# Attention and two MLPs on one core: values of a group loaded by a thread of their own, pooled q and k first, a list ordered with other transfer times

## The chip, the cores and the metric

The kernel runs on one core of one Trainium2 chip. The metric is the device time of one execution in microseconds (us). The core's engines work side by side, each through its own list of instructions in order: TensorE (PE, the matrix products; PEld is its loading of the stationary operand), VectorE (DVE), ScalarE (ACT), GpSimd (POOL), and SyncE (SP, which here issues all DMA transfers). An instruction at the head of an engine's list that waits for another engine or a transfer holds up everything behind it in that list.

## The reference, cut to what matters

```python
# q, k, v: (4, 8, 576, 64); factor 4; scale 1/8
q_d, k_d, v_d = means over 4 neighbouring positions of q, k, v      # (4, 8, 144, 64)
out_up    = repeat(softmax(scale * q_d @ k_d.T) @ v_d, 4)           # pooled attention
scores    = where(abs(i - j) < 4, scale * q @ k.T, -1e9)            # local attention
x         = out_up + softmax(scores) @ v                            # -> (2304, 512)
for w_in, w_out in two layers:                                      # (512, 2048), (2048, 512)
    x = square(relu(x @ w_in)) @ w_out
```

The weights arrive as 64-bit floats. The kernel turns each into two 32-bit parts, a high and a low one, and makes each product of three: high by high, high by low, low by high.

## The kernel before, in words

The 2304 tokens are cut into 9 tiles of 256 (`TN`), the 2048 columns of the hidden layer into 8 parts of 256 (`NP`). A **step** (n, p) of a layer is 24 matmuls for `h` (L695) and 24 for `y` (L730; the second layer has 12 wide ones, L740). Layer 1 begins with tiles 0 and 1 interleaved, tile 1 two parts behind tile 0 (`LEAD`), so that each part of the weights is used twice as soon as it is there; the order starts h(0,0), h(0,1), y(0,0), h(0,2), y(0,1), y(0,2), h(1,0), h(0,3), y(1,0). ACT and DVE make `gH` and `gL` from `h` (L704 to L714) ahead of each y.

The input of layer 1 comes from the attention, for each of 4 batches `b`:

- `pool_qk` (L350), six times: load 384 KB of q or k (L356), add fours on POOL or DVE (L360, L362), transpose on PE (L368), move out by ACT.
- `pool_v` (L332), four times: load 288 KB of v (L337), add fours on POOL (L342, L346) into `vd`.
- `heads_of` (L377), four times, two head pairs at a time (`hd` has two buffers): scores (L389), maximum (L394), exponentials (L399), normalising (L405 to L409), transposes (L416), product with `vd` (L427), result into `outd`. The last product needs all four `pool_v`.
- `group` (L454), five times, 116 query rows each: load q and k rows (L468, two of 256 KB) and the values (L477, four of 64 KB, in pieces of 256 bytes), transposes (L484), masked scores (L499, L508), softmax (L518 to L533), transposes (L537), product with the values (L552), and the addition of the pooled part into the tile `xr` (L566). The product waits for all four `heads_of` of its batch. Tile 0 takes groups 0 to 2 of batch 0, tile 1 groups 2 to 4.

`convert` (L579) turns a quarter of a part of the weights into its two halves: load 512 KB into one of four `ld` buffers (L592 for `w_in`, L597 for `w_out`), ACT L607, DVE L609 and two L612, ACT again, and a subtraction on POOL or DVE (L621). There are 32 for each layer, four for each p, through two buffers `ga`. The `ld` buffers are shared with `pool_qk`, `pool_v`, the groups and the stores. While batch 0 is loaded, buffers of weights not yet filled stand in as more load, value and softmax buffers; rows call those `e`.

The order of all instructions on all engines is made once, when the program is built, by a planner (`Order`): each of the functions above is a thread that yields the engine and the duration it expects, or an event to wait for. Threads stand in lanes; a lane lets so many of its threads be live at a time, in order of a priority given in tiles. The planner starts whatever can start first by its own clock and writes the instruction down. `dma(nbytes)` is its price for a transfer, `dve`, `pool`, `act` those of the engines; where a step offers `[dve(...), pool(...)]` it takes the engine that would be done first. Until the first h it puts matmuls without use (L835, "fills") where it expects PE idle. So numbers in this planner set an order, and no instruction's duration on the chip. The lanes (L821 to L831) are:

```python
    o.lane(3, conversions(1, -0.7, 0.06))
    o.lane(4, groups)
    o.lane(4, heads)
```

Of the kernel before, what the change touches and what calls it, by code (L numbers as in the profile page):

```python
# [20 lines left out]
TN = 256  # L21
# [22 lines left out]
FT = 3  # L44

# [7 lines left out]
class Order:  # L53
# [72 lines left out]
    def run(self):  # L126
        while True:
# [21 lines left out]
            if eng == "SP":  # L149
                self.free[eng] = t + 0.46  # L150
                self.free["DMA"] = max(t + 1.1, self.free.get("DMA", 0.0)) + dur
                value = self.free["DMA"] + 0.95
            else:
                self.free[eng] = t + dur
                value = t + dur + LATENCY[eng]
# [48 lines left out]
def attention_two_mlp_kernel(  # L204
# [96 lines left out]

    def fast(cols):
        return "DVE", 0.165 + cols / 1920.0

    def pool(cols):
        return "POOL", 0.1 + cols * 0.0024
# [10 lines left out]
    def dma(nbytes):  # L317
        return "SP", nbytes / 360e3
# [13 lines left out]
    def pool_v(b, kh, j):  # L332
# [3 lines left out]
        yield dma(72 * 4096)  # L336
# [13 lines left out]
    def pool_qk(b, src, dst, c):  # L350
# [4 lines left out]
        yield dma(128 * 3072)  # L355
# [21 lines left out]
    def heads_of(b, hp):  # L377
# [30 lines left out]
        yield dve(576)  # L408
        nc.vector.tensor_tensor(out=p4, in0=p4, in1=sm.unsqueeze(2).to_broadcast([72, 4, GD]), op=ALU.mult)  # L409
# [32 lines left out]

    x_buf, x_left = {}, {t: TN for t in range(NT)}
# [9 lines left out]

    def group(b, i):  # L454
# [5 lines left out]
        blocks = []  # L460
        for c in range(2):
            qa = q0 + HQ * c
            blocks.append((c, qa, min(HQ, q0 + nq - qa), min(max(0, qa - 3), S - 64)))
        n = yield from f_ld.take(b == 0)
        raw = ld[n].bitcast(F32).rearrange("p (c e) -> p c e", c=2)
        for c, src in enumerate((q, k)):
            yield dma(128 * 2048)
            nc.sync.dma_start(  # L468
                out=raw[:, c].rearrange("p (h d) -> p h d", h=H), in_=src[b, :, r0:r0 + 128].rearrange("h s d -> s h d")
            )  # L470
        nv = yield from f_vw.take(b == 0)
        vw = vw_[nv]
        vj = v[b].rearrange("(h j) s d -> j s h d", j=2)
        for c, _, _, w0 in blocks:
            for j in range(2):
                yield dma(64 * 1024)
                nc.sync.dma_start(out=vw[64 * j:64 * j + 64, c], in_=vj[j, w0:w0 + 64])  # L477
# [25 lines left out]
        tt = yield "PE", 0.35  # L503
# [28 lines left out]
        yield [dve(512), pool(512)]  # L532
# [8 lines left out]
        pT = p.rearrange("p (h c) -> p h c", h=4)  # L541
        yield o.at("heads", b)
# [3 lines left out]
        tt = yield "PE", 0.7  # L546
# [9 lines left out]
        f_vw.put(nv, tt)  # L556
# [22 lines left out]
    def convert(layer, p, kind, half):  # L579
# [8 lines left out]
        if kind == 0:  # L588
            t = ld[n].rearrange("p (k f) -> p k f", k=2)
            fs, ks = slice(p * 256, p * 256 + 256), slice(2 * half, 2 * half + 2)  # L590
            yield dma(64 * 8192)
# [24 lines left out]
        if layer == 1:  # L616
# [3 lines left out]
            tt = yield [dve(512), pool(512)]  # L620
# [8 lines left out]
    def reload(p, kind):  # L629
# [13 lines left out]
        tt = yield [dve(1024), pool(1024)]  # L643
# [16 lines left out]
    def split_x():  # L660
        for n, (layer, t) in enumerate(seq):
# [8 lines left out]
            for c in range(2):  # L670
                ks = slice(2 * c, 2 * c + 2)
                tt = yield [dve(512), pool(512)]
# [135 lines left out]
    heads, groups = [], []  # L808
    for b in range(B):
        t = b * S / TN - 2  # L810
        heads += [(t - 0.1, pool_qk(b, s_, d_, c)) for c in range(3) for s_, d_ in ((q, qd), (k, kd))]
        heads += [(t, pool_v(b, kh, j)) for kh in range(2) for j in range(2)]
        heads += [(t + 0.05, heads_of(b, hp)) for hp in range(4)]
        groups += [((b * S + GQ * i) / TN - 1.9, group(b, i)) for i in range(NG)]
# [12 lines left out]
    o.lane(3, conversions(1, -0.7, 0.06))  # L827
    o.lane(4, groups)
    o.lane(4, heads)
# [60 lines left out]
```

## Time and profile before

| | |
|---|---|
| median of 3 runs | 1008.06 us (1007.47 to 1009.36) |
| the profiled execution, its own time | 1011.32 us |
| span in the profile, first to last instruction | 1009.5 us |
| PE busy | 966.9 us of the span |
| DVE, ACT, POOL busy | 375.9, 454.7, 190.1 us |
| mean granted TensorE clock | 0.981 |
| moved by DMA | 95.62 MB |

The profile's page gives busy times by engine, then 40 slices of the span with the busy share in tenths and the granted clock (PEclk, 9 is nearly full speed; full is 2.4 GHz). The trace can be asked for the busy times of any stretch, for the instructions in order of time, and for what ended each wait. POOL's spans are rough, and a busy PE may run at half clock or do fills, so that both must be looked at beside its busy time.

### The profile page before, as it was taken

The numbers are of one execution on the slowest core, as the hardware profiler recorded it, in microseconds if no ns is written. First come the engines' busy times: TensorE is split into PE (matmuls) and PEld (weight loads), VectorE is DVE, ScalarE is ACT, GpSimd is POOL, SyncE is SP. The second block draws the span as 40 slices with busy tenths as digits, with TensorE's granted clock in tenths as the row PEclk, the third lists the DMA queues.
The fourth block names the chain that finished last, engine by engine and source line by source line (L and its number), as shares of the span: only waits on it lengthen the run. The fifth ranks groups of instructions, "written<-read, shape, count | busy, mean of one in ns | idle before, by whom it ended". The sixth has DMA issues, their size and how long they took to land.

```text
span 1009.5 us, 19268 instructions
## 1 busy us (share of the span) xinstructions
PE 966.9 (96%) x8170; PEld 885.2 (88%) x8170; DVE 375.9 (37%) x651; ACT 454.7 (45%) x885; POOL 190.1 (19%) x170
## 2 busy tenths in 40 slices
PE   6788589999999999999999999999999999999998
PEld 4457589999999999999999998989898989898896
DVE  3698868534647668851111331111111111111110
ACT  3454666445655645543333663333333342424232
POOL 3666433323224101101000331101010100101000
PEclk9799799999999999999999999999999999999999
DMA  8665744326556557640000650101010010101000
GB/s 215 171 171 163 201 143 130 94 65 171 160 157 173 159 179 256 214 157 22 1 22 1 230 187 1 43 1 42 1 43 15 28 43 1 42 1 43 1 22 21
DMA packets 96966, 95.62 MB, mean 95 GB/s; under 512 B 66160, under 2 KB 70768, under 8 KB 96880
## 3 DMA queue, kind: packets, MB, share of 16 engines
q1 hardware_dynamic: 96880, 94.39, 31.1%
q8 instruction: 64, 1.05, 0.4%
q14 instruction: 22, 0.18, 0.1%
HBM read 76.55 MB, written 17.83 MB: 93 GB/s over the span
## 4 chain that ended last, share of the span: by engine, by line
PE 80%; DMA 4%; DVE 2%; ACT 1%; issue 1%; SPq 1%; POOL 0%; ACTq 0%; POOLq 0%
PE h L695 37%; PE y L740 20%; PE y L730 15%; PE at L730 2%; DVE ga L612 1%; DMA ld<-in_moe_w_in_dram 1%; PE at L552 1%; DMA ws<-ga 1%; PE at L484 1%; PE at L508 1%; PE at L427 1%; PE at L389 1%; PE at L416 1%; ACT ga L607 1%; DMA ld<-in_k_dram 1%
## 5 line engine op out<-in xcount | busy, mean ns | idle before, releaser
L695 PE MATMUL h<-xH,w 128*128 128x256 f32 x2304 | 322.8, 282 | 0.0
L695 PEld LDWEIGHTS h<-xH,w 128*128 128x128 f32 x2304 | 296.9, 189 | 8.1 <-issue 1.4
L714 DVE TENSOR_TENSOR gL<-h,gH 128x512 fp32r<-128x512 f32 x144 | 99.3, 690 | 466.7 <-ACT gH L708 466.2
L704 ACT ACTIVATE h<-h 128x512 f32<-128x512 f32 x144 | 83.9, 582 | 355.4 <-PE h L695 355.2
L695 PE MATMUL h<-xL,w 128*128 128x256 f32 x1152 | 182.2, 280 | 0.0
L695 PEld LDWEIGHTS h<-xL,w 128*128 128x128 f32 x1152 | 156.1, 188 | 0.0
L740 PE MATMUL y<-w,gH 128*128 128x512 f32 x576 | 146.1, 394 | 0.0
L730 PE MATMUL y<-gH,w 128*128 128x256 f32 x1024 | 134.2, 283 | 9.1 <-ACT gH L708 9.1
L673 POOL TENSOR_TENSOR xL<-xr,xH 128x512 fp32r<-128x512 f32 x36 | 48.6, 1370 | 498.6 <-ACT xH L315 498.6
L730 PEld LDWEIGHTS y<-gH,w 128*128 128x128 f32 x1024 | 126.0, 190 | 11.2 <-ACT gH L708 9.5
L740 PEld LDWEIGHTS y<-w,gH 128*128 128x128 f32 x576 | 103.3, 187 | 21.0 <-ACT gH L708 0.2
L612 DVE SCALAR_TENSOR_TENSOR ga<-ld,ga 128x512 int32<-128x512 int32 x128 | 102.7, 804 | 2.7
L706 ACT ACTIVATE h<-h 128x512 f32<-128x512 f32 x144 | 84.0, 583 | 3.6
L708 ACT CAST gH<-h 128x512 fp32r<-128x512 f32 x144 | 84.0, 583 | 3.1
L740 PE MATMUL y<-w,gL 128*128 128x512 f32 x288 | 79.0, 395 | 0.0
L730 PE MATMUL y<-gL,w 128*128 128x256 f32 x512 | 73.0, 284 | 0.0
L730 PEld LDWEIGHTS y<-gL,w 128*128 128x128 f32 x512 | 64.9, 189 | 1.0 <-issue 0.6
L740 PEld LDWEIGHTS y<-w,gL 128*128 128x128 f32 x288 | 53.9, 187 | 13.3
L607 ACT ACTIVATE ga<-ld 128x512 f32<-128x512 f32 x64 | 42.8, 669 | 44.0 <-DMA ld<-in_moe_w_in_dram 13.7
L621 POOL TENSOR_TENSOR w<-ga,w 128x512 fp32r<-128x512 f32 x26 | 36.3, 1396 | 59.4 <-ACT w L315 59.2
L609 DVE TENSOR_SCALAR ga<-ga 128x512 int32<-128x512 int32 x64 | 32.5, 508 | 35.9 <-ACT ga L607 35.8
L566 DVE TENSOR_TENSOR xr<-at,outd 64x232 f32<-64x232 f32 (+16 forms) x92 | 32.1, 353 | 24.9 <-PE at L552 23.3
(118 smaller groups left out, 749.2 us busy)
## 6 DMA issues: line engine op xcount, KB each, us to landing
ld<-in_moe_w_in_dram SPq DMA_DIRECT2D x32, 512.0 KB, 4.5
ld<-in_moe_w_out_dram SPq DMA_DIRECT2D x32, 512.0 KB, 4.0
ws<-ga SPq DMA_DIRECT2D x32, 256.0 KB, 4.6
ld<-ws SPq DMA_DIRECT2D x16, 512.0 KB, 3.3
ld<-in_q_dram SPq DMA_DIRECT2D x12, 384.0 KB, 3.5
ld<-in_k_dram SPq DMA_DIRECT2D x12, 384.0 KB, 3.0
ys<-ld SPq DMA_DIRECT2D x9, 512.0 KB, 4.0
xr<-ys SPq DMA_DIRECT2D x9, 512.0 KB, 3.9
```

The lines of the kernel that those rows point to most:

```text
L607: nc.scalar.activation(out=ga[m], in_=wf, func=AF.Copy, scale=2.0 ** -112)
L609: nc.vector.tensor_single_scalar(out=gi, in_=gi, scalar=3, op=ALU.logical_shift_left)
L612: nc.vector.scalar_tensor_tensor(out=gi, in0=w32[:, :, word], scalar=amount, in1=gi, op0=op0, op1=ALU.bitwise_or)
L621: engine().tensor_tensor(out=lo, in0=g, in1=hi.bitcast(F32), op=ALU.subtract)
L673: engine().tensor_tensor(out=xL[n % NXL][:, ks], in0=xr[i][:, ks], in1=xH[n % NXL][:, ks].bitcast(F32), op=ALU.subtract)
L695: nc.tensor.matmul(out=o, lhsT=w[:, kk, fs], rhs=x[:, kk], start=(i == 0), stop=(i == len(mms) - 1))
L704: nc.scalar.activation(out=h, in_=h, func=AF.Relu)
L706: nc.scalar.activation(out=h, in_=h, func=AF.Square)
L708: nc.scalar.copy(gH[i % 2], h)
L714: nc.vector.tensor_tensor(out=gL[i % 2], in0=hb[i % 2], in1=gH[i % 2].bitcast(F32), op=ALU.subtract)
L730: nc.tensor.matmul(out=yb[e // 2][:, (e % 2) * 256:(e % 2) * 256 + 256], lhsT=w[:, fi, e * 128:e * 128 + 128], rhs=g[:, fi * 256:fi * 256 ...
L740: nc.tensor.matmul(out=yb[u], lhsT=g[:, fi * 256 + u * 128:fi * 256 + u * 128 + 128], rhs=w[:, fi], start=beg, stop=end, skip_group_check= ...
```

## The change

Nothing of what is computed is changed. The values of a group get a thread of their own, `values(b, i)`, in a lane that lets one live at a time, with a priority between those of the groups and the pooled parts; the group waits for it only ahead of its product with the values. In the list of pooled parts q and k stand 0.52 tiles ahead of v (0.1 before), the lane of these parts lets six live (four before), the conversions four (three before). The planner prices transfers by the length of their contiguous pieces, 256 to 3072 bytes, an issue of values at 1.2 us on SP, a transfer's landing 1.05 us later, and gives DVE operations with two inputs from SBUF and POOL's a little more; the normalising multiplication of the pooled heads may now go to POOL. Most lines of the changed kernel have other numbers (L389 is L397, L409 is L417, L468 is L490, L477 is L475, L592 is L609).

```diff
+CL, GL, HL = 4, 4, 6
+CP, CD, GP, UP = -0.7, 0, -1.92, -0.78
+QP, VP, HP = -0.52, 0.0, 0.05
...
-                self.free[eng] = t + 0.46
+                self.free[eng] = t + (rows[0] if rows else 0.46)
...
-                value = self.free["DMA"] + 0.95
+                value = self.free["DMA"] + 2.0
...
+    def dve2(cols):
+
+        return "DVE", 0.2 + cols / 720.0
...
-        return "POOL", 0.1 + cols * 0.0024
+        return "POOL", 0.12 + cols * 0.0026
...
-    def dma(nbytes):
-        return "SP", nbytes / 360e3
+    def dma(nbytes, run=4096):
+
+        return "SP", nbytes / (16e3 * run / (8.0 + run * 0.037))
...
-        yield dve(576)
-        nc.vector.tensor_tensor(out=p4, in0=p4, in1=sm.unsqueeze(2).to_broadcast([72, 4, GD]), op=ALU.mult)
+        yield [dve2(576), pool(576)]
+        engine().tensor_tensor(out=p4, in0=p4, in1=sm.unsqueeze(2).to_broadcast([72, 4, GD]), op=ALU.mult)
...
+    def values(b, i):
+        nv = yield from f_vw.take(b == 0)
+        vj = v[b].rearrange("(h j) s d -> j s h d", j=2)
+        for c, _, _, w0 in blocks_of(i):
+            for j in range(2):
+                tt = yield "SP", 0.29, 1.2
+                nc.sync.dma_start(out=vw_[nv][64 * j:64 * j + 64, c], in_=vj[j, w0:w0 + 64])
+        v_of[b, i] = nv
+        ev["vw", b, i] = tt
...
-        yield [dve(512), pool(512)]
+        yield [dve2(512), pool(512)]
...
+        yield o.at("vw", b, i)
+        vw = vw_[v_of[b, i]]
         yield o.at("heads", b)
...
-        heads += [(t - 0.1, pool_qk(b, s_, d_, c)) for c in range(3) for s_, d_ in ((q, qd), (k, kd))]
-        heads += [(t, pool_v(b, kh, j)) for kh in range(2) for j in range(2)]
-        heads += [(t + 0.05, heads_of(b, hp)) for hp in range(4)]
-        groups += [((b * S + GQ * i) / TN - 1.9, group(b, i)) for i in range(NG)]
+        heads += [(t + QP, pool_qk(b, s_, d_, c)) for c in range(3) for s_, d_ in ((q, qd), (k, kd))]
+        heads += [(t + VP, pool_v(b, kh, j)) for kh in range(2) for j in range(2)]
+        heads += [(t + HP, heads_of(b, hp)) for hp in range(4)]
+        vees += [((b * S + GQ * i) / TN + UP, values(b, i)) for i in range(NG)]
+        groups += [((b * S + GQ * i) / TN + GP, group(b, i)) for i in range(NG)]
...
-    o.lane(3, conversions(1, -0.7, 0.06))
-    o.lane(4, groups)
-    o.lane(4, heads)
+    o.lane(CL, conversions(1, CP, CD))
+    o.lane(GL, groups)
+    o.lane(1, vees)
+    o.lane(HL, heads)
```

SP's list, from the fifth transfer on, before (L356 is a load for pooled q or k, L468 rows of q or k of a group, L477 values, L337 v to be pooled, L592 `w_in`; the name ahead of the arrow is the buffer):

```order
L468 DMA e_111<-in_q_dram 128x8x64
L468 DMA e_111<-in_k_dram 128x8x64
L477 DMA vw_86<-in_v_dram 64x4x64 x4
L468 DMA e_112<-in_q_dram 128x8x64
L468 DMA e_112<-in_k_dram 128x8x64
L477 DMA vw_87<-in_v_dram 64x4x64 x4
L468 DMA e_113<-in_q_dram 128x8x64
L356 DMA ld_80<-in_q_dram 128x768
L356 DMA ld_81<-in_k_dram 128x768
L468 DMA e_113<-in_k_dram 128x8x64
L477 DMA e_109<-in_v_dram 64x4x64
L337 DMA e_111<-in_v_dram 72x4x256
```

and the same place with the change (L364, L490, L475, L345 in the same order of meaning):

```order
L364 DMA e_111<-in_q_dram 128x768
L364 DMA e_112<-in_k_dram 128x768
L490 DMA e_113<-in_q_dram 128x8x64
L490 DMA e_113<-in_k_dram 128x8x64
L475 DMA vw_86<-in_v_dram 64x4x64 x2
L490 DMA ld_78<-in_q_dram 128x8x64
L490 DMA ld_78<-in_k_dram 128x8x64
L490 DMA ld_79<-in_q_dram 128x8x64
L345 DMA ld_80<-in_v_dram 72x4x256
L345 DMA ld_81<-in_v_dram 72x4x256
L345 DMA e_111<-in_v_dram 72x4x256
L490 DMA ld_79<-in_k_dram 128x8x64
```

The last two loads of pooled q and k have moved from behind two groups with their values to the fifth and sixth place, and the loads of v to be pooled stand ahead of nearly all values.

Further down SP's list, where the loads for the pooling of batch 1's v (L337) stand among the weights of p = 2 and 3, before:

```order
L597 DMA ld_79<-in_moe_w_out_dram 128x512
L337 DMA ld_78<-in_v_dram 72x4x256
L597 DMA ld_81<-in_moe_w_out_dram 128x512
L337 DMA ld_80<-in_v_dram 72x4x256
L337 DMA ld_78<-in_v_dram 72x4x256
L592 DMA ld_79<-in_moe_w_in_dram 128x2x256
L592 DMA ld_80<-in_moe_w_in_dram 128x2x256
```

and with the change (L609 is `w_in`, L614 `w_out`, L364 pooled q and k of batch 1, L345 its v):

```order
L614 DMA ld_78<-in_moe_w_out_dram 128x512
L609 DMA ld_80<-in_moe_w_in_dram 128x2x256
L364 DMA ld_79<-in_q_dram 128x768
L609 DMA ld_81<-in_moe_w_in_dram 128x2x256
L614 DMA ld_79<-in_moe_w_out_dram 128x512
L364 DMA ld_78<-in_k_dram 128x768
L614 DMA ld_80<-in_moe_w_out_dram 128x512
L345 DMA ld_81<-in_v_dram 72x4x256
```

The two loads of `w_in` for p = 3, the 13th and 14th conversion, stood behind three loads of v; now all four of p = 3 stand ahead of the first one.

POOL's list from the pooling of batch 0's v on, before (L342 and L346 pool v, L533 normalises a group, L360 and L362 pool q or k, L621 makes the low part of a weight):

```order
L342 TENSOR_TENSOR e_111<-e_111 72x4x128
L346 TENSOR_TENSOR vd<-e_111 72x4x64
L342 TENSOR_TENSOR e_112<-e_112 72x4x128
L346 TENSOR_TENSOR vd<-e_112 72x4x64
L533 TENSOR_TENSOR pb_89<-pb_89,nmb_91 128x2x4x64
L342 TENSOR_TENSOR ld_81<-ld_81 72x4x128
L346 TENSOR_TENSOR vd<-ld_81 72x4x64
L342 TENSOR_TENSOR e_111<-e_111 72x4x128
L533 TENSOR_TENSOR e_105<-e_105,nmb_92 128x2x4x64
L346 TENSOR_TENSOR vd<-e_111 72x4x64
```

and with the change (L350 and L354 pool v, L548 normalises a group, L638 makes a low part, L417 normalises a pooled head pair):

```order
L350 TENSOR_TENSOR e_111<-e_111 72x4x128
L350 TENSOR_TENSOR e_113<-e_113 72x4x128
L354 TENSOR_TENSOR vd<-e_111 72x4x64
L354 TENSOR_TENSOR vd<-e_113 72x4x64
L548 TENSOR_TENSOR pb_89<-pb_89,nmb_91 128x2x4x64
L638 TENSOR_TENSOR w_135<-ga_82,w_136 128x512
L417 TENSOR_TENSOR hd_101<-hd_101,nm_103 72x576
L368 TENSOR_TENSOR ld_78<-ld_78 128x3x128
```

The four poolings of v now stand in one piece ahead of the first group's multiplication, and one multiplication of a head pair has come to POOL, behind a step of the first conversion.

## Rows read from the trace of the kernel before

**Rows 1.** The page: busy time by engine, then PE's clock in 40 slices.

```profile
PE 966.9 (96%) x8170; PEld 885.2 (88%) x8170; DVE 375.9 (37%) x651; ACT 454.7 (45%) x885; POOL 190.1 (19%) x170
...
PEclk9799799999999999999999999999999999999999
```

**Rows 2.** Stretches: length, busy PE, PEld, DVE, ACT, POOL, clock, DMA share, GB/s.

```profile
0.00:79.00 79.00, 61.14 (x556) 36.93 (x557) 52.68 (x95) 38.48 (x93) 43.25 (x53) 0.89 0.70 183
79.00:139.00 60.00, 42.71 (x365) 39.96 (x365) 49.76 (x79) 34.53 (x79) 33.36 (x23) 0.83 0.63 182
139.00:225.00 86.00, 86.00 (x931) 82.93 (x929) 49.26 (x92) 44.55 (x84) 23.73 (x21) 1.00 0.35 102
225.00:450.00 225.00, 222.51 (x2471) 211.65 (x2470) 144.31 (x279) 126.45 (x272) 47.16 (x45) 1.00 0.61 182
```

**Rows 3.** The same view for the fills of L835 alone.

```profile
0.00:79.00 79.00, 30.07 (x106) 10.10 (x106) 0.89 0.70 183
```

**Rows 4.** Timeline of PE: start, length, what; a wait ahead in brackets.

```profile
24.73 0.88 PE L389 MATMUL at<-kd,qd 64*72 64x144 f32 x8
...
43.70 1.23 PE L427 MATMUL at<-hd,vd 72*64 72x144 f32 x8
...
46.68 1.24 PE L389 MATMUL at<-kd,qd 64*72 64x144 f32 x8
...
63.10 0.71 PE L427 MATMUL at<-hd,vd 72*64 72x144 f32 x8
...
78.84 1.16 PE L695 MATMUL h<-xH,w 128*128 128x256 f32 x8
```

**Rows 5.** Timeline of SP's queue: issues, with the time each held SP.

```profile
15.59 0.37 SPq L356 DMA_DIRECT2D ld<-in_k_dram  x1
...
22.12 0.62 SPq L592 DMA_DIRECT2D ld<-in_moe_w_in_dram  x1
...
29.15 5.55 SPq L477 DMA_DIRECT2D e<-in_v_dram  x4
```

**Rows 6.** Three more stretches of the same view, within the start.

```profile
2.00:8.00 6.00, 3.21 (x11) 1.50 (x10) 2.92 (x8) 0.80 (x4) 4.87 (x14) 1.00 0.98 309
16.00:36.00 20.00, 14.21 (x156) 8.65 (x146) 15.28 (x29) 10.05 (x29) 10.26 (x10) 0.91 1.03 249
36.00:50.00 14.00, 10.62 (x86) 6.62 (x86) 6.99 (x12) 5.11 (x9) 8.21 (x7) 0.63 0.36 112
```

**Rows 7.** Timeline of DVE: the last pooling of k, and two multiplications.

```profile
20.91 0.56 DVE L360 TENSOR_TENSOR ld<-ld 128x384 f32<-128x384 f32 x1 [3.08 <-DMA ld<-in_k_dram]
...
33.02 1.80 DVE L409 TENSOR_TENSOR hd<-hd,nm 72x576 f32<-72x576 f32 x1
...
37.29 2.50 DVE L409 TENSOR_TENSOR hd<-hd,nm 72x576 f32<-72x576 f32 x1
```

**Rows 8.** Timeline of POOL: the pooling of v, beside those.

```profile
32.95 1.26 POOL L342 TENSOR_TENSOR ld<-ld 72x512 f32<-72x512 f32 x1 [1.16 <-DMA ld<-in_v_dram]
34.29 3.67 POOL L346 TENSOR_TENSOR vd<-ld 72x256 f32<-72x256 f32 x1
...
40.66 0.73 POOL L346 TENSOR_TENSOR vd<-e 72x256 f32<-72x256 f32 x1
```

**Rows 9.** Groups of the whole span, by shape: count, busy us, mean ns, idle before.

```profile
L342 POOL TENSOR_TENSOR e<-e 72x512 f32<-72x512 f32 x3 | 3.8, 1265 | 4.3 <-DMA e<-in_v_dram 2.5 <-PE y L389 1.9
...
L533 DVE TENSOR_TENSOR pb<-pb,nmb 128x512 f32<-128x512 f32 x11 | 8.9, 810 | 0.4
L533 POOL TENSOR_TENSOR pb<-pb,nmb 128x512 f32<-128x512 f32 x6 | 7.6, 1263 | 64.2 <-DVE nmb L531 50.0 <-DVE nm L396 14.2
```

**Rows 10.** What stood in the way at 100 us: PE, ACT, and a wait of SP.

```profile
108.61 3.78 PE L730 MATMUL y<-gH,w 128*128 128x256 f32 x16 [8.48 <-ACT gH L708]
...
102.21 0.66 ACT L607 ACTIVATE ga<-ld 128x512 f32<-128x512 f32 x1 [5.66 <-DMA ld<-in_moe_w_in_dram]
...
SPq L592 <- POOL vd L346: 5.9, 1, 5.9
```

More of the change, by code (lines that the diff above doesn't have):

```diff
@@ L335, in pool_v @@
         t = lf.rearrange("p (h r d) -> p h r d", h=4, r=4)
-        yield dma(72 * 4096)
+        yield dma(72 * 4096, 1024)
         nc.sync.dma_start(
@@ L354, in pool_qk @@
         t = lf[:, 0:768].rearrange("p (g r d) -> p g r d", g=3, r=4)
-        yield dma(128 * 3072)
+        yield dma(128 * 3072, 3072)
         nc.sync.dma_start(
@@ L440, in heads_of @@
         count(("heads", b), 4, tt)
+    v_of = {}
     x_buf, x_left = {}, {t: TN for t in range(NT)}
@@ L452, in x_tiles, with blocks_of @@
             yield lambda: 0.0 if x_buf[t] is not None else None
+    def blocks_of(i):
+        q0 = GQ * i
+        nq = min(GQ, S - q0)
+        return [(c, qa, min(HQ, q0 + nq - qa), min(max(0, qa - 3), S - 64)) for c, qa in enumerate((q0, q0 + HQ))]
+    def values(b, i):
[7 more added lines that the diff above has]
+        ev["vw", b, i] = tt
     def group(b, i):
@@ L459, in group @@
         r0 = min(max(0, q0 - 3), S - 128)
[L460 to L463, printed above, removed]
+        blocks = blocks_of(i)
         n = yield from f_ld.take(b == 0)
@@ L466, in group @@
         for c, src in enumerate((q, k)):
-            yield dma(128 * 2048)
+            yield dma(128 * 2048, 256)
             nc.sync.dma_start(
@@ L470, in group @@
             )
[L471 to L477, printed above, removed]
         m = yield from f_qk.take(b == 0)
@@ L502, in group @@
             )
-        tt = yield "PE", 0.35
+        tt = yield "PE", 0.5
         for hp in range(4):
@@ L545, in group @@
         a = yield from f_at.take()
-        tt = yield "PE", 0.7
+        tt = yield "PE", 0.9
         xp = pair[a].rearrange("p j (h c) -> p j h c", h=4)
@@ L555, in group @@
                     )
-        f_vw.put(nv, tt)
+        f_vw.put(v_of[b, i], tt)
         f_pb.put(u, tt)
@@ L590, in convert @@
             fs, ks = slice(p * 256, p * 256 + 256), slice(2 * half, 2 * half + 2)
-            yield dma(64 * 8192)
+            yield dma(64 * 8192, 2048)
             nc.sync.dma_start(out=t, in_=w_in.rearrange("(k p) f -> p k f", p=128)[:, ks, fs])
@@ L619, in convert @@
             evac(hi, g)
-            tt = yield [dve(512), pool(512)]
+            tt = yield [dve2(512), pool(512)]
             engine().tensor_tensor(out=lo, in0=g, in1=hi.bitcast(F32), op=ALU.subtract)
@@ L642, in reload @@
         evac(hi, tv)
-        tt = yield [dve(1024), pool(1024)]
+        tt = yield [dve2(1024), pool(1024)]
         engine().tensor_tensor(out=lo, in0=tv, in1=hi.bitcast(F32), op=ALU.subtract)
@@ L671, in split_x @@
                 ks = slice(2 * c, 2 * c + 2)
-                tt = yield [dve(512), pool(512)]
+                tt = yield [dve2(512), pool(512)]
                 engine().tensor_tensor(
@@ L806, in leave @@
             ev["stored", n] = tt
-    heads, groups = [], []
+    heads, groups, vees = [], [], []
     for b in range(B):
         t = b * S / TN - 2
-        heads += [(t - 0.1, pool_qk(b, s_, d_, c)) for c in range(3) for s_, d_ in ((q, qd), (k, kd))]
-        heads += [(t, pool_v(b, kh, j)) for kh in range(2) for j in range(2)]
-        heads += [(t + 0.05, heads_of(b, hp)) for hp in range(4)]
-        groups += [((b * S + GQ * i) / TN - 1.9, group(b, i)) for i in range(NG)]
+        heads += [(t + QP, pool_qk(b, s_, d_, c)) for c in range(3) for s_, d_ in ((q, qd), (k, kd))]
[3 more added lines that the diff above has]
+        groups += [((b * S + GQ * i) / TN + GP, group(b, i)) for i in range(NG)]
     def conversions(layer, t0, dt):
```

## The prediction

> **What bounds the kernel now.** I read the page first. PE is busy 966.9 us of a span of 1009.5, and its clock dips only in the first slices [rows 1]. The stretches then say where time can still be won: from 139 to 225 us PE is busy without a gap at the full clock, from 225 to 450 it lacks 2.5 us of 225 [rows 2], and the page's later slices show the full clock. So PE bounds everything behind 139 us. In the first 79 us PE looks busy for 61.14 us, but 30.07 of that are fills [rows 2, 3]; only 31.1 us are of use, so 48 us are lost. From 79 to 139 PE is busy 42.71 of 60 us at a mean clock of 0.83 [rows 2]: 17.3 us idle and some more in slow matmuls. The first h starts at 78.84 [rows 4]. The reader should see a long start, limited by something other than PE, and then a wall of PE work; a change of the order can win only in the start.
>
> What sets the start? The chain ends in all four head pairs of batch 0, because no product with a group's values may run before them. The first pair's scores start at 24.73, its last product at 43.70; the second pair's scores start at 46.68 and the last product at 63.10; from there the products with the values, the additions into tile 0 and its splitting take until 78.84 [rows 4]. The first scores needed the last pooled k, which went out on SP at 15.59 [rows 5] and ended DVE's wait at 20.91 [rows 7]. The first product needed the pooled v, whose last addition ended at 40.66 + 0.73 = 41.39 [rows 8]. So both early dates come from the place in the list of transfers. From 16 to 36 us the transfer engines are busy all the time, at 249 GB/s with pieces of mixed length; from 2 to 8, where mostly pooled parts with long pieces run, they move 309 GB/s [rows 6].
>
> A second stop lies at 100 us: PE waits 8.48 us for gH, since ACT stands 5.66 us at the conversion of a weight that has not landed, and SP had held that load 5.9 us for the buffer of a pooled v of batch 1 [rows 10].
>
> **The change part by part.**
>
> *Pooled q and k first.* The six loads are 6 x 393,216 bytes = 2.36 MB. Counting from 2 us at 309 GB/s [rows 6] they have landed at 2 + 7.6 = 9.6 us; with a microsecond for landing, some 10.5, against 20.91 before [rows 7]. From that point to the first scores it was 24.73 - 20.91 = 3.8 us. One more group's transposes and scores stand ahead of them on PE now, 1 to 2 us by estimate. Scores at 15.5 to 16: about 9 us earlier.
>
> *Pooled v ahead of the values.* Through the fourth of these loads the list now holds 5.24 MB (2.36 of pooled parts and 2.88 of q, k, v and two values); 9.6 + 2.88/0.249 = 21.2 us. POOL then needs 1.27 and 0.73 us for each [rows 8, 9] and can do the first two while the others land: vd ready at 21.2 + 2 x 2.0 = 25 instead of 41.39. From the first scores to the first product it was 19.0 us [rows 4], in which PE's list also waited for vd and for a group's k. With those two out of the way I keep 12 to 14 by estimate: product at 28 to 30, and the second pair's scores, 3.0 us behind it before [rows 4], at 30 to 33. From the second scores to the last product 16.4 us, from that to the first h 15.7 us [rows 4], both kept: 30 + 16.4 + 15.7 = 62 and 33 + 32.1 = 65 are the ends for the first h, taken as 63. That is 16 us earlier.
>
> *First conversions.* The first w_in went out at 22.12 [rows 5]. Now 6.16 MB stand in the list through it: 9.6 + 3.80/0.249 = 24.9 us to land, so about as before; the third and fourth quarters, split before by a group and its values (SP 5.55 us on four of them [rows 5]), stand together now. Cost nil; it is hidden as long as the heads come later.
>
> *Batch 1's v behind the weights of p = 3.* The 13th and 14th load no longer wait for POOL's vd. The 8.48 us wait at y(0,2) [rows 10] loses its cause. What is late next is the conversion itself: DVE is busy 49.76 of 60 us from 79 to 139, so 83% [rows 2]. Conversions start about 8 to 12 us earlier, not 16, so with h(0,2) 16 us earlier y(0,2) will still wait some microseconds. I book no gain beyond the 16 us: the wait only must not grow. From y(0,2) to 139 the same work is left, and I keep its 30 us.
>
> *Multiplications moved to POOL.* No row shows L409 on POOL; the nearest are L533 there, 1.263 us for 512 columns, and L342's 1.265 [rows 9]. I take 1.4 for 576, with ends of 1.27 and 2.5 (what L409 took beside a busy POOL [rows 7]). Up to the 22nd conversion two of these go to POOL: 2 x 1.4 there, and 2 x 0.8 off DVE (L533's price there, 0.810 [rows 9]). Net between -1.6 and +3.4 us, on a path that has just gained 16; taken as 0.
>
> What the rows show here speaks against moving work: L409 at 33.02 took 1.80 us beside an L342 on POOL, the one at 37.29 took 2.50, and L346 on POOL 3.67 beside DVE's work, when another took 0.73 [rows 7, 8]. The Trainium skill, "SBUF — State Buffer", section "SBUF: two separate sides", says why: DVE operations with two SBUF inputs and POOL's operations take one shared port for a whole instruction each, so the other stands. These rows agree with it. By that rule the two moves would cost 2 x (1.4 - 0.8) = 1.2 us of port instead of nothing.
>
> *Behind 139 us.* Values come by a single thread. PE's list has a product with values for each of 15 later groups; a late value would stop the wall. Bounds: 0, and a share of SP's 5.55 us for each (below). Taken as 0, as in the 225 us of rows 2 only 2.5 us are lost, and the values are asked for well ahead of a softmax that takes longer than they do.
>
> Sum: -16 us, ends -4 (only conversions count, and moves cost 3.4) and -27 (the 8.48 us wait goes as well, and a little more). Against the profiled execution's own 1011.32 us that is 995.3; the median of the runs is 3.3 us lower, 1008.06, and the same 16 us there give 992.
>
> **The rivals.**
>
> *POOL and DVE hold each other up, and the start is as long as their common work.* For it: the stretched operations of rows 7 and 8 and DVE's 83%. Then only what moves into idle time counts: four poolings of v, 4 x (1.27 + 0.73) = 8.0 us, less 1.2 for the two moved multiplications: 7 us, 1001 us. Against: from 36 to 50 us DVE was busy 6.99 and POOL 8.21 of 14 us [rows 6], so both also stood for lack of work. The skill's rule named above is this mechanism.
>
> *The stop at 100 us goes entirely.* If the conversions keep pace, 8.48 us come on top of 16: 983.5. For it: the order no longer holds these loads; against: DVE.
>
> *Nothing happens.* The same bytes must land and the same conversions be made before the wall; were the start bound by them alone, the order of the heads would not matter: 1007.
>
> *Late values stop the wall: slower.* Place: PE's product with values (L569 now) in batches 1 to 3, where the transposes behind it on PE wait too. If each of 15 waits a quarter of the 5.55 us that four values took on SP [rows 5], 1.4 us, it is 21 us against the 16 won: 1013. It decides from 16/15 = 1.1 us a group.
>
> **How the numbers follow.** Forecast (988 to 997) 0.45; the gone stop 0.16; POOL and DVE 0.22; nothing 0.07; late values 0.10. About 0.2% is what a measurement can tell from no change here. Faster 0.45 + 0.16 + 0.22 = 0.83, same 0.07, slower 0.10. The range leaves out the slower case, the 0.07 in which nothing happens, and a few hundredths at its lower end: 980 to 1005.
>
> **What would show it.** The first scores at 15 to 17 us, vd complete before 28, the first h at 60 to 66, fills under 25 us, PE without gap from about 123 us on, and the stretch behind it with no more than 3 us of waits. It is wrong if the first h starts after 74 us, if the wait at y(0,2) is over 16 us, or if products with values wait in the later batches.

## The result, and the profile after

The changed kernel takes 994.65 us (median of 4 runs, 994.42 to 995.86), the kernel before beside it 1008.71 (4 runs, 1007.47 to 1009.8): a ratio of 0.9863, with a 95% interval of 0.9846 to 0.9881. The profiled execution took 994.6 us (1011.32 before), with a span of 992.7 (1009.5). So 14.1 us went by the medians and 16.7 between the two profiled executions. The profiled execution of the kernel before is slower than all four of its timed runs, so differences read from the two traces are some 3 us larger than those of the medians.

The page of the kernel after, busy time by engine and PE's clock in 40 slices, against [rows 1]:

```profile
PE 955.6 (96%) x8152; PEld 879.4 (89%) x8152; DVE 381.2 (38%) x637; ACT 456.5 (46%) x885; POOL 205.9 (21%) x184
...
PEclk9988799999999999999999999999999999999999
```

Stretches of the kernel after (columns as in [rows 2]), and the fills alone, L854 now:

```profile
0.00:79.00 79.00, 63.57 (x644) 43.34 (x644) 62.84 (x115) 45.47 (x106) 47.46 (x55) 0.94 0.77 214
79.00:139.00 60.00, 43.34 (x367) 41.45 (x368) 54.19 (x71) 35.66 (x80) 36.66 (x28) 0.83 0.54 167
139.00:225.00 86.00, 86.00 (x933) 82.93 (x932) 38.42 (x77) 44.64 (x88) 26.90 (x27) 1.00 0.36 101
225.00:450.00 225.00, 225.00 (x2499) 214.56 (x2498) 131.48 (x261) 123.31 (x264) 52.57 (x50) 1.00 0.57 168
36.00:50.00 14.00, 13.02 (x134) 7.97 (x133) 13.87 (x23) 9.79 (x27) 10.94 (x9) 1.00 0.54 155
```

```profile
0.00:79.00 79.00, 24.28 (x88) 8.52 (x88) 0.94 0.77 214
```

The wall behind 139 us is as dense as before, and the 2.5 us that PE lacked from 225 to 450 us are gone. Where did the time go? PE's busy time fell by 966.9 - 955.6 = 11.3 us, its idle time by 16.8 - 11.3 = 5.5. Of the 11.3, 30.07 - 24.28 = 5.8 us were fills. The rest, 5.4 us, is the same 8064 other matmuls: they took 936.8 us and now take 931.4. By the clock's records 27.7 us of them ran at the lower level, 1.2 GHz, in the start before, and 17.8 us run there now. Eight matmuls of h take 1.91 us at 114.03, at that level, and 1.10 at 120.78; by that ratio 4 of the 5.4 us, by estimate, are what the lower level cost more before. So a third of the gain between the two traces is less idle time, a third fewer fills, and a third the same matmuls, mostly because fewer of them ran at the lower clock.

DVE was busy 52.68 + 49.76 = 102.4 us up to 139 us before [rows 2] and is 117.0 now, so its idle time fell from 36.6 to 22.0 us. From 36 to 50 us it was busy 6.99 us [rows 6] and now is 13.87.

The chain of the pooled heads on PE (L397 their scores, L435 their product with pooled v, L712 h), and the stops of PE that are left:

```profile
15.28 0.71 PE L397 MATMUL y<-kd,qd 64*72 64x144 f32 x8
...
28.36 0.71 PE L435 MATMUL at<-hd,vd 72*64 72x144 f32 x8
...
31.85 0.71 PE L397 MATMUL at<-kd,qd 64*72 64x144 f32 x8
...
46.82 0.71 PE L435 MATMUL y<-hd,vd 72*64 72x144 f32 x8
...
63.91 1.80 PE L712 MATMUL h<-xH,w 128*128 128x256 f32 x8
...
92.49 0.85 PE L376 MATMUL at<-ident,ld 128*64 128x128 f32 x3 [6.06 <-POOL ld L370]
92.99 3.48 PE L747 MATMUL y<-gH,w 128*128 128x256 f32 x16
...
110.43 1.15 PE L424 MATMUL at<-ident,hd 72*72 72x72 f32 x8 [10.28 <-DVE hd L417]
```

Against [rows 4], the first scores come 9.5 us sooner, the first product 15.3, the last 16.3 and the first h 14.9. The stop of 8.48 us for gH [rows 10] is gone; in its place PE waits 6.06 us for pooled rows of batch 1 and, later, 10.28 us ahead of the transposes of batch 1's heads. From 110.43 on PE has no gap up to 985 us. From 79 to 139 us PE is idle 16.7 us, against 17.3 before: this stretch comes earlier but is no denser.

DVE and POOL ahead of that last stop (L629 merges the words of a weight, L350 pools v of batch 1):

```profile
102.85 4.55 DVE L629 SCALAR_TENSOR_TENSOR ga<-ld,ga 128x512 int32<-128x512 int32 x2
```

```profile
102.65 2.50 POOL L350 TENSOR_TENSOR ld<-ld 72x512 f32<-72x512 f32 x2 [2.10 <-DMA ld<-in_v_dram]
105.11 1.73 POOL L638 TENSOR_TENSOR w<-ga,w 128x512 fp32r<-128x512 f32 x1
```

and all 53 such mergings up to 139 us (minimum, median and maximum in ns):

```profile
L629 DVE SCALAR_TENSOR_TENSOR ga<-ld,ga x53: 672/693/2854, 30.6 to 138.4; 128x512 int32<-128x512 int32 x53
```

The median is 0.69 us, the mean 1.00. So part of DVE's 90% in 79 to 139 us is not work but waiting inside an instruction. The same group up to 139 us, before (L612) and after, with its busy time and mean:

```profile
L612 DVE SCALAR_TENSOR_TENSOR ga<-ld,ga 128x512 int32<-128x512 int32 x43 | 39.1, 912 | 0.6
```

```profile
L629 DVE SCALAR_TENSOR_TENSOR ga<-ld,ga 128x512 int32<-128x512 int32 x53 | 52.7, 1000 | 1.0
```

Of the 14.6 us by which DVE's busy time rose, 13.6 lie here; ten more mergings at 0.69 us are 6.9. About half of the rise is therefore longer waiting, so DVE's busy time up to 139 us overstates what it got done.

### The profile page after: what moved, and what is told of

It is laid out like the page before. It is cut to its first block, busy times and chain, and to the rows that moved or that the text cites. A ratio compares the mean times of both kernels' runs of the same rounds, so it can differ in the third digit from the quotient of the medians.

```text
span 992.7 us, 19264 instructions
## 1 busy us (share of the span) xinstructions
PE 955.6 (96%) x8152; PEld 879.4 (89%) x8152; DVE 381.2 (38%) x637; ACT 456.5 (46%) x885; POOL 205.9 (21%) x184
## 3 DMA queue, kind: packets, MB, share of 16 engines
q8 instruction: 64, 1.05, 0.4%
## 4 chain that ended last, share of the span: by engine, by line
PE 88%; DVE 1%; ACT 0%; ACTq 0%; issue 0%
PE h L712 41%; PE y L757 20%; PE y L747 18%; PE at L747 2%; PE at L569 2%; PE at L499 1%; PE at L523 1%; PE at L435 1%; PE at L424 1%; PE at L552 1%; PE at L397 1%; DVE ga L629 1%; PE at L376 0%; PE at L514 0%; DVE w L638 0%; DVE ga L626 0%
## 5 line engine op out<-in xcount | busy, mean ns | idle before, releaser
L712 PE MATMUL h<-xH,w 128*128 128x256 f32 x2304 | 324.5, 283 | 0.0
L712 PEld LDWEIGHTS h<-xH,w 128*128 128x128 f32 x2304 | 298.1, 190 | 8.6 <-issue 2.1
L712 PE MATMUL h<-xL,w 128*128 128x256 f32 x1152 | 183.4, 281 | 0.0
L712 PEld LDWEIGHTS h<-xL,w 128*128 128x128 f32 x1152 | 157.3, 190 | 0.0
L690 POOL TENSOR_TENSOR xL<-xr,xH 128x512 fp32r<-128x512 f32 x31 | 40.7, 1331 | 474.1 <-ACT xH L322 474.1
L629 DVE SCALAR_TENSOR_TENSOR ga<-ld,ga 128x512 int32<-128x512 int32 x128 | 105.4, 826 | 2.8 <-DVE ga L626 0.2
L638 POOL TENSOR_TENSOR w<-ga,w 128x512 fp32r<-128x512 f32 x27 | 39.3, 1458 | 48.9 <-ACT w L322 48.7
L810 ACT COPY ld<-y 128x512 f32<-128x512 f32 x34 | 18.6, 590 | 50.5 <-PE y L757 34.2
```

The lines of the kernel that those rows point to most:

```text
L629: nc.vector.scalar_tensor_tensor(out=gi, in0=w32[:, :, word], scalar=amount, in1=gi, op0=op0, op1=ALU.bitwise_or)
L638: engine().tensor_tensor(out=lo, in0=g, in1=hi.bitcast(F32), op=ALU.subtract)
L690: engine().tensor_tensor(out=xL[n % NXL][:, ks], in0=xr[i][:, ks], in1=xH[n % NXL][:, ks].bitcast(F32), op=ALU.subtract)
L712: nc.tensor.matmul(out=o, lhsT=w[:, kk, fs], rhs=x[:, kk], start=(i == 0), stop=(i == len(mms) - 1))
```

## The experiments

Two theories stood at first. The prediction's: the place of the pooled parts in the list of transfers sets the date of the first h, and all else follows it (in the texts, "place in the list", later H). Its rivals: the thread of values, the prices, or the work moved off DVE. All kernels below change the kernel after, except the two that start from the kernel before. In the table the "22nd weight" is the end of the 22nd of the 32 subtractions that finish layer 1's weights, counted in the timelines of POOL and DVE. "PE without use" is PE's idle time up to 139 us and its fills together, "the matmuls" the busy time of the 8064 others. Each ratio is to the kernel before timed beside that run; its median was 1005.15 to 1008.71 us there, so differences of 1 or 2 us between rows show little.

| kernel | ratio to before (95%) | first h, us | 22nd weight, us | DVE busy to 139 us | PE busy of 139 to 225 | PE without use to 139 us | the matmuls, us |
|---|---|---|---|---|---|---|---|
| before | 1 | 78.8 | 144.2 | 102.4 | 86.0 | 65.2 | 936.8 |
| after | 0.9863 (0.9846 to 0.9881) | 63.9 | 126.7 | 117.0 | 86.0 | 56.4 | 931.4 |
| before, lane of heads 6 | 1.0024 (1.0004 to 1.0044) | 67.4 | 150.9 | 102.7 | 79.7 | 58.2 | 937.5 |
| before, both lanes | 0.9978 (0.9956 to 1.0001) | 68.2 | 134.4 | 104.5 | 86.0 | 58.6 | 935.5 |
| after, lane of heads 4 | 0.9946 (0.9923 to 0.9969) | 74.3 | 124.8 | 111.5 | 80.6 | 55.7 | 933.3 |
| after, values in the group | 0.9916 (0.9885 to 0.9948) | 65.2 | 130.5 | 113.6 | 86.0 | 60.9 | 931.5 |
| after, conversions as before | 0.9881 (0.9835 to 0.9927) | 60.8 | 135.3 | 114.6 | 86.0 | 56.3 | 931.0 |
| after, L417 on DVE | 0.9878 (0.9836 to 0.992) | 65.8 | 128.7 | 116.6 | 86.0 | 58.2 | 931.5 |
| after, 8 mergings twice | 0.9945 (0.993 to 0.996) | 67.1 | 134.7 | 117.1 | 86.0 | 63.4 | 932.1 |
| after, no v additions in batch 1 | 0.9843 (0.9824 to 0.9863) | 65.9 | 122.8 | 113.8 | 86.0 | 53.5 | 930.6 |
| after, small DVE steps out | 0.9876 (0.9842 to 0.991) | 64.1 | 125.4 | 115.8 | 86.0 | 55.5 | 930.5 |
| after, batch 1 behind h(1,0) | 1.0056 (1.0033 to 1.008) | 58.9 | 119.9 | 111.6 | 66.9 | 50.2 | 940.0 |
| after, batch 1 behind h(1,2) | 1.0065 (1.005 to 1.008) | 59.2 | 117.2 | 114.5 | 71.0 | 52.2 | 939.5 |
| after, heads of batch 1 behind h(1,1) | 0.9957 (0.9937 to 0.9977) | 64.9 | 126.4 | 113.2 | 80.4 | 54.4 | 936.7 |

### The place of the pooled parts, alone and undone

```diff
 # the kernel before, one lane
-    o.lane(4, heads)
+    o.lane(6, heads)
```

> The kernel before with one number changed: the lane of the pooled parts lets six threads live instead of four. Its list of transfers then begins with all six loads of pooled q and k, and the four loads of v to be pooled stand at places 12 to 16, without the thread of values, the new prices or the multiplication on POOL. Theory (the time is won by the place of the pooled parts in the list): first scores of the pooled heads at 15 to 17 us, first h at 62 to 67, 992 to 998 us. Rival (the thread of values and the new prices carry it; the four values of a group stand ahead of the pooled v here): first product of the pooled heads not before 34 us, first h after 70, 1001 us or more.

The first h came 11.5 us sooner, at 67.38, and the time did not fall: 1.0024. So the date of the first h is not enough; the prediction's theory falls as it stood. Three rows of this run show what went against it. SP's queue issues the first load of w_in (L592) only now:

```profile
29.80 0.55 SPq L592 DMA_DIRECT2D ld<-in_moe_w_in_dram  x1
```

8.9 us after its place in the kernel after (20.91), behind 15 of the 16 loads of values of four groups; and in the stretch from 16 to 36 us DVE is short of work:

```profile
16.00:36.00 20.00, 13.98 (x163) 9.56 (x163) 9.60 (x19) 7.68 (x24) 9.78 (x9) 0.74 0.90 224
```

9.60 us, against 15.28 before [rows 6]; the 22nd weight is 6.7 us later than before. The third is in the wall:

```profile
139.00:225.00 86.00, 79.67 (x859) 76.67 (x858) 57.38 (x102) 46.56 (x83) 32.73 (x27) 0.96 0.42 130
```

Up to 139 us PE spends 65.2 - 58.2 = 7.0 us less without use than before, so the early heads did win time there; then it stands 6.3 us, in the longest waits ahead of a group's scores (2.56 us at 167.93) and of its transposes (1.97 us behind DVE at 178.99). That the late conversions left DVE this work is likely, but no run shows it.

```diff
-CL, GL, HL = 4, 4, 6
+CL, GL, HL = 4, 4, 4
```

> The changed kernel with the lane of the pooled parts back at four threads; all else stays. The last two loads of pooled q and k then stand behind three groups' rows, 4.1 MB into the list instead of 2.4, and the last load of v to be pooled behind two loads of w_in, 7.3 MB into it. Theory (place in the list): first scores near 20 us, first product of the pooled heads 33 to 36, first h 68 to 72, 999 to 1004 us. Rival (the thread of values and the new prices carry the gain): within 2 us of the changed kernel, 993 to 997.

The opposite case: the weights are as early as in the kernel after (124.8 against 126.7), the first h is 10.4 us later, at 74.32, and 0.9946 - 0.9863 = 0.8% of the time comes back (7.0 us by the medians, 1001.69 against 994.65). The time that the theory expected came, but not by its way: up to 139 us PE spends 55.7 us without use, no more than in the kernel after (56.4). The loss stands later, at groups that wait for DVE and ACT:

```profile
198.00:208.00 10.00, 5.20 (x85) 4.40 (x84) 4.33 (x11) 3.78 (x6) 4.43 (x5) 0.85 0.24 66
```

PE is idle 4.8 of these 10 us, and 5.8 in all behind 139 us. The lane of six is needed, then; that it is needed for the first h, this run does not show, as the lane holds the pooled parts of all four batches.

### The thread of values, and the lanes

```diff
+        yield from values(b, i)
...
-        vees += [((b * S + GQ * i) / TN + UP, values(b, i)) for i in range(NG)]
...
-    o.lane(1, vees)
```

> The changed kernel with the loading of a group's values put back into the group, ahead of its transposes; lanes and prices stay new. Pooled q, k and v keep their early places in the list. Theory (place in the list): first h within 2 us of the changed kernel's 63.9, time 993 to 998 us. Rival (the thread of values is what frees the start): first h after 68 us, 999 us or more.

The first h stayed (65.2), and yet 0.5% came back, 5 us; neither expectation fits. The loss lies in the start: 60.9 us of PE without use up to 139, against 56.4. The values of three groups again stand ahead of the first w_in, which this run issues at 27.20 instead of 20.91, and the 22nd weight ends 3.8 us later. What the thread of values buys is not an earlier first h; the early weights are what is left, though the run does not set them apart from the rest of the list.

```diff
-CL, GL, HL = 4, 4, 6
-CP, CD, GP, UP = -0.7, 0, -1.92, -0.78
+CL, GL, HL = 3, 4, 6
+CP, CD, GP, UP = -0.7, 0.06, -1.92, -0.78
```

> The changed kernel with the lane of conversions as before (three live, later parts 0.06 tiles behind each other) and all else new. The first 25 transfers stay in their order, so the first h should start within 2 us of 63.9. Theory D: if the fourth live conversion is what keeps DVE supplied, its idle time up to 139 us rises from 22 to 26 to 30 us and the time by as much, 998 to 1003. Theory H: within 2 us of the changed kernel.

No difference that this shows (0.9881, 993.75 us): the time that theory H expected, and not theory D's. The weights are 8.6 us later here, but PE does other useful work in their place: from 79 to 139 us it runs 457 matmuls instead of 367, the attention of batch 1 among them, which the kernel after does later. DVE's idle time, 139 - 114.6 = 24.4 us, is close to the 22.0 of the kernel after. So the date of the weights alone is not the measure either.

```diff
 # the kernel before, two lanes
-    o.lane(3, conversions(1, -0.7, 0.06))
+    o.lane(4, conversions(1, -0.7, 0))
...
-    o.lane(4, heads)
+    o.lane(6, heads)
```

> The kernel before with both lanes of the changed one, conversions four live without the 0.06, pooled parts six live; thread of values, prices and multiplication as before. With the pooled parts' lane alone DVE was busy 102.7 us up to 139 us, and the time did not move. If the lanes carry the change: DVE busy 110 us or more up to 139, 996 to 1002 us. If the thread of values or the prices are needed (the first w_in stands at place 24 here, at 20 in the changed kernel): DVE busy under 106 us, 1004 to 1010.

0.9978: the lanes alone give nearly nothing. DVE's 104.5 us are where the second expectation put it, and the 1003.42 us lie just under its time. Yet its first h (68.2) and its 22nd weight (134.4) are both some 10 us earlier than in the trace of the kernel before. So these two dates together do not make the gain either; against the kernel after this run has 2.2 us more of PE without use up to 139 us, 2.0 us of idle time behind it, and 4.1 us more in the same matmuls. Between this run (0.9978) and the one with the values in the group (0.9916) stand the planner's new prices and priorities, and the multiplication on POOL. No run tries the prices alone, and what they carry stays open.

### DVE's time, put to the test

These runs suggested theory D: until layer 1's weights are converted, what counts is how much of its work DVE has behind it, conversions and attention together.

```diff
             nc.vector.scalar_tensor_tensor(
                 out=gi, in0=w32[:, :, word], scalar=amount, in1=gi, op0=op0, op1=ALU.bitwise_or
             )
+            if layer == 1 and 1 <= p <= 2 and word:
+                nc.vector.scalar_tensor_tensor(
+                    out=gi, in0=w32[:, :, word], scalar=amount, in1=gi, op0=op0, op1=ALU.bitwise_or
+                )
```

> The changed kernel, every list in its order, but in the eight conversions of p = 1 and 2 DVE does the first of its two mergings of words twice (the second time it changes nothing). In the changed kernel 53 such mergings take 1.00 us each up to 139 us, so this adds 8 us of DVE's work between 50 and 95 us. Theory D, formed after the first four runs (until the weights of layer 1 are converted, DVE's time is what the start is made of: from before to after DVE's idle time up to 139 us fell from 36.6 to 22.0 us, and the four runs so far line up with it): 6 to 9 us longer than the changed kernel, 1001 to 1004. Theory H (the chain of the pooled heads alone sets the start, conversions have slack): 0 to 2 us longer, 995 to 997.

0.9945 against 0.9863: 0.8%, 8 us, as much as the eight mergings cost at 1.00 us each; the spans differ by 1000.5 - 992.7 = 7.8. With every list in its order, an operation more on DVE between 50 and 95 us goes into the time one for one, and theory H's slack in the conversions is ruled out. PE's time without use up to 139 us rises by as much, from 56.4 to 63.4. (The operation lengthens each conversion as well as DVE's list; the run does not part the two, but DVE was busy all the same: 62.37 of 79 us and 54.71 of the 60 behind.)

```diff
-        engine().tensor_tensor(out=p4, in0=p4, in1=sm.unsqueeze(2).to_broadcast([72, 4, GD]), op=ALU.mult)
+        nc.vector.tensor_tensor(out=p4, in0=p4, in1=sm.unsqueeze(2).to_broadcast([72, 4, GD]), op=ALU.mult)
```

> The changed kernel, every list in its order, but the normalising multiplications of the pooled heads that went to POOL are done by DVE at the same place. Two of them lie ahead of 139 us. Theory (the start is not won there): within 2 us of the changed kernel, 993 to 997. Rival A (DVE bounds 79 to 139 us, so that each move took 0.8 us off it and more beside a busy POOL): 997 to 1000. Rival B (the port that both engines share costs more than DVE saves): 991 to 993, and the wait of 10.28 us at the transposes near 110 us shrinks by over 1 us.

0.9878, inside the interval of the kernel after: the multiplications moved to POOL carry at most a small part, as the first theory expected.

```diff
-        nc.gpsimd.tensor_tensor(out=t[:, :, 0:2], in0=t[:, :, 0:2], in1=t[:, :, 2:4], op=ALU.add)
+        if b != 1:
+            nc.gpsimd.tensor_tensor(out=t[:, :, 0:2], in0=t[:, :, 0:2], in1=t[:, :, 2:4], op=ALU.add)
...
+        if b != 1:
+            nc.gpsimd.tensor_tensor(out=vd[:, 4 * j:4 * j + 4, kh], in0=t[:, :, 0], in1=t[:, :, 1], op=ALU.add)
```

> The changed kernel without POOL's eight additions that pool the v of batch 1 (their result is left out, so batch 1 uses the sums of batch 0); all else and every order stay. In the changed kernel they lie beside DVE's two mergings at 102.85 us that take 4.55 us together, ahead of the multiplication for which PE waits 10.28 us. If a shared port stretches DVE: these two take under 2.8 us, the wait shrinks by 2 to 4 us, and the time by 1 to 4, to 991 to 994. If the two merely run beside each other: no change, 994 to 996.

The two mergings that took 4.55 us, in DVE's timeline without POOL's additions beside them, and PE's wait after them:

```profile
103.34 1.42 DVE L631 SCALAR_TENSOR_TENSOR ga<-ld,ga 128x512 int32<-128x512 int32 x2
```

```profile
PE at L426 <- DVE hd L419: 6.0, 1, 6.0
```

1.42 us, and 6.0 instead of 10.28. So POOL's additions stretch DVE's mergings. The Trainium skill, "SBUF — State Buffer", section "SBUF: two separate sides", has it that of a DVE operation with two SBUF inputs and a POOL operation that reads SBUF the one that starts first holds a shared port pair for its whole length, and the other waits; these rows (4.55 us beside the additions, 1.42 without) agree. For the time the run settles less: 0.9843 and 992.14 us, 2.5 us under the kernel after, with intervals that overlap.

```diff
-        nc.vector.tensor_scalar(out=sm, in0=sm, scalar1=1e-9, scalar2=4.0, op0=ALU.add, op1=ALU.mult)
...
-        nc.vector.tensor_scalar_add(sm, sm, 1e-9)
...
-        evac(
+        nc.scalar.activation(
             out=outd[b % 2][:, hp].rearrange("p (g r) -> p g r", r=2),
-            in_=pair[a][:, 0, 288:432].unsqueeze(2).to_broadcast([128, GD, 2]),
+            in_=pair[a][:, 0, 288:432].unsqueeze(2).to_broadcast([128, GD, 2]), func=AF.Copy, scale=0.25,
```

> The changed kernel, all lists in its order, without two small operations of DVE's: the addition of 1e-9 to a sum of exponentials whose largest is 1 (nothing is left of it in 32 bits), and the factor 4 on that sum for the pooled heads, which ACT applies as 0.25 when it moves the heads' result out. Up to 139 us these are six operations of 0.76 us and five of 0.39 in the changed kernel, 6.5 us of DVE's time, or 1.5 by the shortest among them (0.13 to 0.2 us), if the rest is only waiting that other work would inherit. Theory D (DVE's time until the weights are converted is what the start is made of): 2 to 6 us less than the changed kernel, 989 to 993, and a little less than before in the later stretches at most. Theory H (only the head chain of batch 0): 0 to 1 us less.

No difference: 994.44 us against 994.65, which is theory H's expectation and not theory D's. Of the 6.5 us taken out, DVE's busy time up to 139 us fell by only 117.0 - 115.8 = 1.2. A small operation's 0.76 us was then mostly waiting, and other operations now hold it: the mergings' mean went from 1.00 to 1.03 us.

### The stop that is left: batch 1 later

```diff
     def pool_qk(b, src, dst, c):
+        if b == 1:
+            yield o.at("h", 1, 0)
...
     def group(b, i):
+        if b == 1:
+            yield o.at("h", 1, 0)
```

> The changed kernel with one more wait in the planner: pooled q and k and the groups of batch 1 ask for nothing before h(1,0). So batch 1's loads, its poolings (some 22 us of POOL), transposes and heads (some 5 us of DVE) leave the stretch from 60 to 120 us and stand among the later steps, where DVE was busy 38 of 86 us. Theory D: conversions come sooner, PE's waits of 6.06 us at the pooled q of batch 1 and of 10.28 us at its heads go, 5 to 12 us less than the changed kernel: 983 to 990. Theory H (the head chain of batch 0 alone): within 2 us of it, 993 to 997. Rival (the later batches come late and stop the wall): over 998.

The first half of theory D's expectation came: the first h at 58.9, the 22nd weight 6.8 us earlier, 50.2 us of PE without use up to 139 instead of 56.4, the two waits for batch 1 gone (one of 9.1 us for gH in their place). But the time is 2.0% longer than that of the kernel after. PE from 139 to 225 us in this run:

```profile
139.00:225.00 86.00, 66.91 (x666) 59.55 (x668) 38.53 (x68) 38.98 (x91) 33.03 (x32) 0.84 0.35 97
```

19 us idle, and the clock at 0.84 in the mean. Batch 1 is owed to tile 2, and it is a long chain; held back, it stops the wall. The next run, with `"h", 1, 2` for `"h", 1, 0`, says the same:

> The same with the wait on h(1,2), about three steps of 7 us later. Theory D: as the run that waits for h(1,0) or up to 3 us better, 981 to 989, so long as tile 2 does not wait. Rival (batch 1 late for tile 2): a wait at the first h of tile 2 or at the products with its values, and slower than the run that waits for h(1,0) by 3 us or more.

1.0065. Its weights come 2.7 us earlier still, and the loss is in the same stretch (71.0 of 86 us). The two are equal within their intervals, and both some 25 us above what theory D expected.

```diff
     def heads_of(b, hp):
+        if b == 1:
+            yield o.at("h", 1, 1)
```

> The changed kernel with one more wait in the planner: the pooled heads of batch 1 (their scores, softmax and products, not the poolings) ask for nothing before h(1,1). PE's transposes that wait 10.28 us for DVE at 110 us then stand about two steps later. Theory D, by now: DVE with POOL on its port sets the pace up to 139 us, and that wait is only where it shows; the wait goes, another at a weight's conversion (gH or w ahead of h or y) of 6 to 10 us takes its place, and the time stays within 3 us of the changed kernel, 992 to 998. Rival W (the wait itself is the loss): 5 to 10 us less, 985 to 990. Rival L (batch 1 now late for tile 2, as in the runs that held all of batch 1 back): PE loses time between 139 and 225 us, over 999.

Here the poolings stay and only the heads wait. The stop of 10.28 us goes, but PE from 79 to 139 us gains just 46.05 - 43.34 = 2.7 us of work, and behind it loses more:

```profile
79.00:139.00 60.00, 46.05 (x374) 44.43 (x374) 50.54 (x72) 33.88 (x72) 34.18 (x26) 0.89 0.52 167
139.00:225.00 86.00, 80.42 (x830) 75.63 (x830) 39.70 (x73) 42.42 (x86) 18.78 (x18) 0.94 0.31 90
```

0.9957, so 9 us longer than the kernel after: rival L, by its place and its price. Of this and the other runs none beats the kernel after beyond the intervals.

Of theory D this leaves less than its name says. The time that it expected came in one run, the mergings done twice; it did not come with the conversions as before, with the small operations out, or with batch 1 or its heads held back. Shown is that more work in the conversions of p = 1 and 2 costs its own length; that DVE's busy time as such sets the time is not.

## Why the prediction was right, and where it was not

**The heads' dates** held: first scores 15.28 (15.5 to 16 predicted), first product 28.36 (28 to 30), second scores 31.85 (30 to 33), first h 63.91 (63). Pooled v was 2.7 us late. POOL's timeline, its first addition and its last:

```profile
18.30 2.61 POOL L350 TENSOR_TENSOR ld<-ld 72x512 f32<-72x512 f32 x2 [7.27 <-DMA ld<-in_v_dram]
...
25.75 1.95 POOL L354 TENSOR_TENSOR vd<-e 72x256 f32<-72x256 f32 x2
```

The step let POOL do two of the four while the others land; but the first landed at 18.30, and all four then ran without a gap until 27.7, at 2.35 us each instead of 2.0. Ahead of them SP had been held 5.26 us by two issues of values:

```profile
5.05 5.26 SPq L475 DMA_DIRECT2D vw<-in_v_dram  x2
```

The product's date had room for that.

**The first conversions** were booked at nothing, w_in being as early as before. It was (issued at 20.91, 22.12 before [rows 5]). Two runs suggest that this "nothing" was a condition of the gain: with the first w_in 6 us later (values in the group) a third of it was gone, and with w_in 9 us later (the heads' lane alone, where other parts of the change are missing too) all of it. The step named the cover ("hidden as long as the heads come later"); with the heads early the weights are no longer hidden.

**The stop at 100 us** was forecast to lose its cause and to stay in some other form, with no gain beyond 16 us. That is what the trace shows, at other places: 6.06 us at L376 and 10.28 at L424 in place of 8.48 at gH. The step expected the next stop at a conversion; the largest stands at batch 1's heads instead. The conversions, booked as 8 to 12 us earlier, are 3.4 us earlier at the second weight (46.6 to 43.2) and 17.5 at the 22nd.

**The multiplications on POOL** took 1.18 and 1.50 us (1.4 taken), and the net of 0 was right to within what the run resolves.

**Behind 139 us** PE has no gap (from 110.43 on; 123 predicted), 225.00 of 225 us in the long stretch, and no product with values waits there: the late values, the slower case, did not come. Fills fell to 24.28 us (under 25).

**The sum** of -16 stands against -14.1 by the medians and -16.7 between the profiled executions. So the number holds, and the dates of the heads behind it hold too. The step from there to the time, an earlier first h counted one for one, came out here (14.9 us of first h, 14.1 of time) but is no rule: with the heads' lane alone an 11.5 us earlier first h won nothing, and with the lane of four a 10.4 us later one cost PE nothing up to 139 us. In the trace, PE's time without use up to 139 us fell by 65.2 - 56.4 = 8.8 us; the rest is 2.5 us of gaps behind 225 us and 5.4 us in the same matmuls, for which the sum has no term. That these add up to about 16 is in part luck.

Of the rivals, the one with POOL and DVE in each other's way gave a time too long (1001), but its mechanism is at work, as the mergings show that took 4.55 us beside POOL's additions and 1.42 without them. "Nothing happens" is what the heads' lane alone does, though not for that rival's reason alone: PE won time in the start there and lost it behind 139 us.

What stays open: which part of the change carries how much, the planner's prices above all, which no run tried alone; and how much of the time the shared port costs in all. Up to 139 us the mergings alone take 53 x (1.00 - 0.69) = 16 us more than their median would give; only the additions of batch 1 were taken away, and their effect on the time is within the intervals.

## What to carry to other kernels

Where a start is made of several chains, the date at which one of them ends is no measure of the time. Add up what the engine of the later wall loses in the whole start (idle time, matmuls without use, matmuls at the lower clock), and look whether the wall behind it stays dense: four runs here that won time in the start lost it again to a later batch. A wait is often just where the pace shows: moved away, it came back elsewhere, here larger. What is "free" because something later hides it stops being free once that something is made earlier.

## What the runs showed of the hardware

- DVE's mergings of 128x512 took 0.69 us in the median and up to 2.85 beside POOL. Of the 53, the 21 that no operation of POOL overlaps took 0.67 to 0.69 us; all the longer ones had one beside them. The waiting stands inside the instruction's time, so a busy DVE is no measure of its work.
- What an issue of values holds SP is no fixed price: two of them took 5.26 us at 5 us, with eight loads of 256 or 384 KB just issued, and one took 0.61 at 25.9:

```profile
25.90 0.61 SPq L475 DMA_DIRECT2D vw<-in_v_dram  x1
```

- A stop of PE costs more than its length: behind the 6.06 us at 92.49 the 16 matmuls of y took 3.48 us, against 1.98 in the step ahead of it. The granted clock of the stretch is 0.77 in the mean, so a part of it ran at the lower level, 1.2 GHz:

```profile
83.55 1.98 PE L747 MATMUL y<-gH,w 128*128 128x256 f32 x16
```

```profile
79.00:110.00 31.00, 14.76 (x138) 13.84 (x138) 28.13 (x38) 16.16 (x41) 22.20 (x18) 0.77 0.50 158
```
